# Another place for tile 5's transposed scores, and a written-out order of work, in a fused attention and softplus-FFN kernel

## The chip, the cores and the metric

One core of a Trainium2 chip runs the whole program. The metric is the device time of one launch in microseconds (us), as the median of several runs. The engines are named PE (TensorE), DVE (VectorE), ACT (ScalarE), POOL (GpSimd) and SP (SyncE, which here only issues DMAs).

## The reference, cut to what matters

```python
B, H, S, D = 8, 8, 576, 64          # chunks of 64 along S
scores = matmul(q_c, k_c.T) / sqrt(D)
attn = exp(scores - max(scores)); attn = attn / (sum(attn) + 1e-09)
x = matmul(attn, v_c)               # -> x (4608 x 512)
h = x @ w_in                        # w_in 512 x 2048
g = softplus(h)
out = g @ w_out                     # w_out 2048 x 512
```

All of it is float32; only chunks on the diagonal are computed.

## The kernel before, in words

**Matmuls in parts.** Each float32 factor of the FFN is split into a high and a low part, and three products (hi·hi, hi·lo, lo·hi) take the place of one. The weights arrive raw and are decoded once, in 32 units u: `w_load` (L309), `w_top` (L325), `w_low`, `w_add`, `w_hi` and `w_lo`. Raw weights pass through a ring of three buffers. The first units decode into `stage` (L257), four buffers called `wib`, each of which holds four units of 512 columns.

**Attention.** The 4608 tokens are 36 tiles i of 128. Tiles 0 to 3 are prepared on PE at the start. For the others, VectorE transposes q into a `qe` buffer and k into a `ka` buffer (`blk_t`, L539, tasks Tq and Tk; two `ka` buffers in all). PE computes the scores (`blk_s`, L556), VectorE takes the maximum and subtracts it (max, sub), ScalarE does the exponential, and VectorE or GpSimd the division. The probabilities must then be transposed: for most tiles VectorE does it wholly (`blk_e4`). Tile 5 is one of the few others: VectorE transposes 32x32 blocks with one instruction (`blk_e`, L575, task Te5), whose output lies in the tile's own key buffer `ka`, and eight DMAs of SP's queue move the blocks to their places in `eT` (`blk_swap`, L593, task swap5). PE then multiplies `eT` with v (L653), ScalarE writes the high part of x (xh) and VectorE the low part (xl).

**Bursts.** From tile 4 on PE does attention in bursts between FFN blocks: `burst` (L672) does the values of an earlier tile and the scores of a later one, once for each of a pair. Burst 8 has the values of tile 4 and the scores of tile 6 in its first half (B8_0), the values of tile 5 and the scores of tile 7 in its second (B8_1). Each half takes one of two `pa` banks of PSUM, which the first GEMM's outputs take in turn with it.

**FFN.** Nine blocks m of 512 tokens, sixteen slices fc of the hidden width. For the first three blocks each pair (m, fc), numbered g, is G1 (`gemm1`, L681), softplus on ScalarE (`sp_g`, L704, task sp), high part (hi), low part (lo) and G2 (`gemm2`, L911). The other six go in three supers of two blocks, whose G1 is done by seven products P0 to P6 for each pair of slices, in a Strassen-like scheme: VectorE and GpSimd combine results (`mix`), ScalarE copies some of them out of PSUM (`hold`, L868, tasks s1, e) and takes the softplus of others (`soft`, L895), and what cannot be used at once is spilled to memory (`spill_store`, L900). Final passes multiply the spilled part.

**The order.** Tasks are registered with `Plan.add`, each with its engine, cost, needs and urgency. `Plan.order` (L60) plays through these costs and chooses the order of each engine's instructions by urgency; `Plan.emit` (L146) then moves single tasks by two hand-written lists. An engine runs its instructions in that order. `keep_warm` (L421) puts matmuls of the identity matrix, whose result nobody reads, ahead of a task where the play-through leaves PE a gap early on:

```python
for _ in range(int(FILL * (plan.gap - 0.6) / 0.23)):
    nc.tensor.matmul(dst[:, :P], ident, ident, start=True, stop=True)
```

Tile 7's key transpose Tk7 writes into the buffer that tile 5's scores lie in until swap5 has moved them, so its needs hold swap5 (L1403):

```python
keep = [f"S{FIRST_BLK - 1}"] if ps == F else [f"Te{i - 2}" if n == "q" else swapped[i - 2]]
```

Of the kernel before, what the change touches and what calls it, by code (L numbers as in the profile page):

```python
# [33 lines left out]
class Plan:  # L34


    CROSS = 0.15
    OWN = 0.08
    TABLE = 1.28
    RATE = 265e3  # L40
    FLYING = 8
    AHEAD = 3.2
    WARM_UNTIL = 90.0
    HOLD = 0.55
    HOLD_FROM = 120.0

    def __init__(self, **pools):
        self.tasks, self.gap = {}, 0.0
        self.pools = {n: (c, []) for n, c in pools.items()}

    def add(
        self, name, eng, cost, fn, needs=(), urg=0.0, table=None, take=(), kb=0, slack=0.0, after=(), port=False, parts=1,
        late={}, room={}
    ):
        self.tasks[name] = dict(
            name=name, eng=eng, cost=cost, fn=fn, needs=list(needs) + list(after), after=set(after), urg=urg, table=table,
            take=take, kb=kb, slack=slack, seq=len(self.tasks), port=port or eng == "POOL", parts=parts, late=late, room=room,
        )

    def order(self):  # L60
        T = self.tasks
        kids, left, ready = {}, {}, {}
        for t in T.values():
            left[t["name"]] = len(t["needs"])
            for n in t["needs"]:
                kids.setdefault(n, []).append(t["name"])
        fin, issued, free, tab, dma_free, port = {}, {}, {}, None, 0.0, 0.0
        wait, landed = {}, {}
        times = [0.0]

        def known(t):
            r = t["slack"] if not t["needs"] else 0.0
            for n in t["needs"]:
                if n in t["after"]:
                    r = max(r, issued[n])
                    continue
                same = T[n]["eng"] == t["eng"] and not T[n]["kb"]
                lat = (0.0 if t["eng"] == "PE" else self.OWN) if same else self.CROSS + t["slack"]
                r = max(r, fin[n] + lat - t["late"].get(n, 0.0))
            ready[t["name"]] = r  # L80
            wait.setdefault(t["eng"], []).append(t)
            heapq.heappush(times, r)

        def has_room(t, now):
            for at, (pool, _) in enumerate(t["take"]):
# [11 lines left out]
        out = []  # L97
# [1678 lines left out]
```

## Time and profile before

| what | value |
|---|---|
| median of 3 runs | 822.53 us (821.55 to 823.56) |
| span of the profiled execution | 818.6 us |
| runs' median less that span | 3.9 us |
| PE busy | 809.0 us, 99% of the span |
| VectorE, ScalarE, GpSimd busy | 563.6, 391.4, 406.6 us |
| granted PE clock, mean | 0.998 |

The profiled execution is known by its span, from its first to its last instruction. A busy PE is not yet a PE at its peak: filler matmuls count as busy, and records of pipelined matmuls overlap, so that start times tell more than idle times. Line numbers are those of the kernel before.

### The profile page before, as it was taken

The numbers are of one execution on the slowest core, as the hardware profiler recorded it, in microseconds if no ns is written. First come the engines' busy times: TensorE is split into PE (matmuls) and PEld (weight loads), VectorE is DVE, ScalarE is ACT, GpSimd is POOL, SyncE is SP. The second block draws the span as 40 slices with busy tenths as digits, with TensorE's granted clock in tenths as the row PEclk, the third lists the DMA queues.
The fourth block names the chain that finished last, engine by engine and source line by source line (L and its number), as shares of the span: only waits on it lengthen the run. The fifth ranks groups of instructions, "written<-read, shape, count | busy, mean of one in ns | idle before, by whom it ended". The sixth has DMA issues, their size and how long they took to land.

```text
span 818.6 us, 16629 instructions
## 1 busy us (share of the span) xinstructions
PE 809.0 (99%) x6186; PEld 687.5 (84%) x6186; DVE 563.6 (69%) x914; ACT 391.4 (48%) x635; POOL 406.6 (50%) x512
## 2 busy tenths in 40 slices
PE   9999999999999999999999999999999999999997
PEld 7787888888888888888888888888888888999997
DVE  3998985357557687376769887376784646798773
ACT  4877765444443564354446545363542434443431
POOL 1555569776988643867857474336204550000000
PEclk9999999999999999999999999999999999999999
DMA  9987767764475455898897589886529998953421
GB/s 221 238 218 199 210 159 216 226 147 123 90 190 125 114 149 199 223 265 251 213 235 201 164 266 313 235 240 210 182 100 305 345 369 323 413 186 128 134 76 52
DMA packets 216482, 168.90 MB, mean 206 GB/s; under 512 B 153936, under 2 KB 186704, under 8 KB 215504
## 3 DMA queue, kind: packets, MB, share of 16 engines
q1 hardware_dynamic: 201648, 117.75, 50.0%
q0 software_dynamic: 14208, 49.56, 20.0%
q8 instruction: 49, 0.80, 0.4%
q10 hardware_dynamic: 544, 0.52, 0.2%
q14 instruction: 33, 0.27, 0.1%
HBM read 115.87 MB, written 50.86 MB: 204 GB/s over the span
## 4 chain that ended last, share of the span: by engine, by line
PE 88%; DMA 3%; DVE 3%; POOL 2%; ACT 2%; SPq 1%; issue 1%; DVEq 0%; POOLq 0%; ACTq 0%
PE po L922 28%; PE pa L863 21%; PE pa L690 14%; PE pa L1065 8%; PE po L1065 6%; PE po L863 5%; PE pa L653 2%; PE pa L565 1%; PE po L423 1%; DMA raw<-in_moe_w_in_dram 1%; DMA xa<-in_q_dram 1%; DMA tails<-xa 1%; DMA raw<-in_moe_w_out_dram 1%; SPq L534 0%; DVE wib L889 0%
## 5 line engine op out<-in xcount | busy, mean ns | idle before, releaser
L922 PE MATMUL po<-late,g_hi 128*128 128x512 f32 x360 | 110.3, 393 | 0.0
L863 PE MATMUL pa<-wib,xb 128*128 128x512 f32 x360 | 85.9, 392 | 0.0
L863 PEld LDWEIGHTS pa<-wib,xb 128*128 128x128 f32 x360 | 66.9, 188 | 15.8 <-ACT wib L869 1.8
L922 PEld LDWEIGHTS po<-late,g_hi 128*128 128x128 f32 x360 | 66.7, 188 | 14.6 <-DVE late L376 0.3
L863 PE MATMUL pa<-wi_hi,xb 128*128 128x512 f32 x240 | 73.9, 389 | 0.0
L922 PE MATMUL po<-wo_hi,g_hi 128*128 128x512 f32 x192 | 72.1, 394 | 0.0
L922 PE MATMUL po<-wo_hi,g_lo 128*128 128x512 f32 x192 | 71.4, 391 | 0.2 <-DVE g_lo L714 0.2
L922 PE MATMUL po<-wo_lo,g_hi 128*128 128x512 f32 x192 | 71.2, 390 | 0.0
L922 PE MATMUL po<-late,g_lo 128*128 128x512 f32 x192 | 70.9, 390 | 0.0
L706 ACT ACTIVATE u<-pa 128x512 f32<-128x512 f32 (+1 forms) x48 | 28.3, 589 | 83.0 <-PE pa L690 76.5
L818 POOL DMA_DIRECT2D xb<-scratch x58 | 35.9, 620 | 60.7 <-PE pa L863 57.8
L889 DVE TENSOR_TENSOR wib<-wib,pa 128x512 f32<-128x512 f32 x64 | 44.0, 687 | 28.9 <-PE pa L863 16.7
L897 ACT ACTIVATE ends<-pa 128x512 f32<-128x512 f32 x40 | 24.0, 599 | 78.6 <-PE pa L863 41.4
L863 PEld LDWEIGHTS pa<-wi_hi,xb 128*128 128x128 f32 x240 | 45.1, 188 | 9.7 <-issue 0.3
L589 DVE STREAM_TRANSPOSE eT<-qe 32x256 f32<-32x256 f32 x112 | 48.9, 436 | 2.6
L889 POOL TENSOR_TENSOR wib<-wib 128x512 f32<-128x512 f32 x32 | 42.0, 1311 | 17.1 <-ACT wib L869 16.4
L869 ACT COPY wib<-pa 128x512 f32<-128x512 f32 x52 | 29.7, 587 | 43.3 <-PE pa L863 43.3
L889 DVE TENSOR_TENSOR wib<-pa,wib 128x512 f32<-128x512 f32 x24 | 16.6, 690 | 45.8 <-ACT ends L897 23.8
L690 PE MATMUL pa<-xb,wib 128*128 128x512 f32 x192 | 46.5, 390 | 0.3 <-DVE wib L376 0.2
L863 PE MATMUL pa<-wi_lo,xb 128*128 128x512 f32 x120 | 46.7, 389 | 0.1
L714 POOL TENSOR_TENSOR g_lo<-u,g_hi 128x512 fp32r<-128x512 f32 x23 | 31.0, 1347 | 24.6 <-ACT g_hi L710 24.5
L922 PEld LDWEIGHTS po<-wo_hi,g_lo 128*128 128x128 f32 x192 | 36.0, 188 | 8.5 <-DVE g_lo L714 1.0
(370 smaller groups left out, 2075.7 us busy)
## 6 DMA issues: line engine op xcount, KB each, us to landing
xb<-scratch POOLq DMA_DIRECT2D x38, 512.0 KB, 5.6
spill<-ends SPq DMA_DIRECT2D x35, 512.0 KB, 5.5
xb<-scratch POOLq DMA_DIRECT2D x20, 768.0 KB, 7.0
ends<-spill SPq DMA_DIRECT2D x21, 512.0 KB, 3.3
out_dram<-raw SPq DMA_DIRECT2D x34, 256.0 KB, 3.4
raw<-in_moe_w_in_dram SPq DMA_DIRECT2D x16, 512.0 KB, 5.2
raw<-in_moe_w_out_dram SPq DMA_DIRECT2D x16, 512.0 KB, 4.6
scratch<-ends SPq DMA_DIRECT2D x16, 512.0 KB, 3.4
```

The lines of the kernel that those rows point to most:

```text
L589: nc.vector.transpose(live["eT", i][d : d + BL, tb], e[s : s + BL, 1 - tb])
L653: nc.tensor.matmul(pa[o, a, col : col + C], vt[r, 4 * j + 2 * h2 + c2, :], eT[r, :, 4 * c2 + 2 * j + h2, :], start=True, stop=True,)
L690: nc.tensor.matmul(ph, wt[:, c, :], x[:, ts_, c, :], start=(n == 0), stop=(n == 3 * KC - 1))
L706: nc.scalar.activation(w["u"], w["ph"], AF.Softplus)
L714: (nc.gpsimd if pool else nc.vector).tensor_tensor(w["lo"], w["u"], w["hi"].bitcast(F32), op=ALU.subtract)
L818: on("ring").dma_start(to[:, here], src[:, cut])
L863: nc.tensor.matmul(w["bank"][BANK[k]], wts[:, q, c, :], x[:, c, :], start=k < NX and c + n == 0, stop=c == 1 and n == 2, skip_group_check= ...
L869: nc.scalar.copy(tmp_of(n), w["bank"][n])
L889: (nc.gpsimd if what in MIX_POOL and w["s"] < LAST else nc.vector).tensor_tensor(out, a, b, op=op)
L897: nc.scalar.activation(u_tiles(j)[i], src, AF.Softplus)
L922: nc.tensor.matmul(pos[w["m"]][t], terms[n][0][:, j * P : (j + 1) * P], terms[n][1], start=(w["first"] and n == 0), stop=n == 2 and w["last"],
L1065: nc.tensor.matmul(f_bank(k)[:, t * HW : (t + 1) * HW], x[:, t * P : (t + 1) * P], wt, start=j == n == t == 0, stop=j == 7 and n == 2 and ...
```

## The change

Three things change. Tile 5's transposed scores (Te5) are written into the first 512 columns of the third staging buffer, and swap5 reads them there; Tk7 now needs the second half of burst 4 (the last reader of tile 5's key) in place of swap5. Te5 needs the decoded units of that buffer to be done, and one later weight step that writes there needs swap5. Second, the play-through and all urgencies are gone: a string `ISSUED` names all tasks in one order, which is each engine's order. Third, keep-warm matmuls are counted by a table instead of from the gaps of the play-through.

```diff
     def keep_warm(dst):
-        for _ in range(int(FILL * (plan.gap - 0.6) / 0.23)):
+        for _ in range(plan.warm):
             nc.tensor.matmul(dst[:, :P], ident, ident, start=True, stop=True)
-        plan.gap = 0.0
+        plan.warm = 0
...
     def blk_s(i, pa):
...
+        ea = stage[EA_STAGE[i]][:, :DM] if i in EA_STAGE else ea
         live["eA", i] = ea.rearrange("p (u h k) -> p u h k", u=2, h=H)
...
+    EA_STAGE = {5: 2}
...
                 keep = [f"S{FIRST_BLK - 1}"] if ps == F else [f"Te{i - 2}" if n == "q" else swapped[i - 2]]
+                if n == "k" and i - 2 in EA_STAGE:
+                    keep = [f"B{at_of[ps - 1]}_{i % 2}"]
...
+                staged = [f"w_{a_}{u_}" for a_ in ("hi", "lo") for u_ in range(4 * EA_STAGE[i], 4 * EA_STAGE[i] + 4)] if i in EA_STAGE else []
+                plan.add(f"Te{i}", "DVE", 0.65, partial(blk_e, i), [f"norm{i}"] + staged)
...
+    for i, n in EA_STAGE.items():
+        name = f"w_hi{of_in[HALF_FC + 4 * (n // 2)]}"
+        MOVED.append((name, {"needs": plan.tasks[name]["needs"] + [f"swap{i}"]}))
...
-    plan.emit(MOVED, BEHIND, AHEAD, in_turn)
+    WARM = {'T0': 15, 'S0': 3, 'E2': 3, 'V2': 2}
+    ISSUED = """
...
+    plan.emit(ISSUED.split(), MOVED, WARM, in_turn)
```

PE's order around burst 8, before (L690 is the first GEMM, L653 the values, L565 the scores, L423 the keep-warm matmuls, L922 the second GEMM):

```order
L690 MATMUL pa_963<-xb_370,wib_953 128x512 x4
L653 MATMUL pa_983<-eT_893,xa_105 64x64 x16
L565 MATMUL pa_983<-ka_957,qe_951 64x64 x16
L423 MATMUL pa_1044<-ident_86 128x128 x6
L653 MATMUL pa_1044<-eT_938,xa_105 64x64 x16
L565 MATMUL pa_1044<-ka_1039,qe_978 64x64 x16
L922 MATMUL po0_542<-wo_hi_101,g_hi_949 128x512
```

And with the change, where L568 is the first GEMM, L531 the values, L442 the scores and L800 the second GEMM:

```order
L568 MATMUL pa_966<-xb_370,wib_920 128x512 x4
L531 MATMUL pa_993<-eT_890,xa_105 64x64 x16
L442 MATMUL pa_993<-ka_981,qe_964 64x64 x16
L531 MATMUL pa_1042<-eT_928,xa_105 64x64 x16
L442 MATMUL pa_1042<-ka_988,qe_959 64x64 x16
L800 MATMUL po0_531<-wo_hi_101,g_hi_955 128x512
```

The six keep-warm matmuls between the halves of burst 8 are gone. Nothing else differs in PE's order from the first instruction to the last, and SP's order is the same except that swap5 reads `wib` instead of `ka`.

VectorE's order around tile 7's key, before (L541 is a key or query transpose, L345 a `w_add`, L610 a maximum, L615 its subtraction, L376 a `w_lo`, L670 an xl step; `ka_1039<-xa_105` is Tk7, `xa_1097<-pa_983` is xl4):

```order
L376 TENSOR_TENSOR wib_954<-ends_106,wib_953 128x512
L376 TENSOR_TENSOR wo_lo_102<-ends_106,wo_hi_101 128x512
L541 STREAM_TRANSPOSE qe_978<-xa_105 128x512
L345 ISA ends_106<-ends_106 128x1024 x2
L541 STREAM_TRANSPOSE ka_1039<-xa_105 128x512
L345 ISA ends_106<-ends_106 128x1024
L610 TENSOR_REDUCE mx_1102<-pa_983 128x8
L615 TENSOR_TENSOR qe_951<-pa_983,mx_1102 128x512
L376 TENSOR_TENSOR late_1023<-ends_106,late_1022 128x512
L670 TENSOR_TENSOR xa_1097<-pa_983,xa_1096 128x4x2x64
```

And with the change (L418, L222, L488, L493, L253 and L548 in the same roles; `ka_988<-xa_105` is Tk7, `xa_1090<-pa_993` is xl4):

```order
L222 ISA ends_106<-ends_106 128x1024
L418 STREAM_TRANSPOSE ka_981<-qk_116 128x512
L222 ISA ends_106<-ends_106 128x1024
L418 STREAM_TRANSPOSE ka_988<-xa_105 128x512
L253 TENSOR_TENSOR late_991<-ends_106,late_990 128x512
L488 TENSOR_REDUCE mx_1093<-pa_993 128x8
L548 TENSOR_TENSOR xa_1090<-pa_993,xa_1089 128x4x2x64
L493 TENSOR_TENSOR qe_964<-pa_993,mx_1093 128x512
```

Tk7 stands one step ahead of the `w_lo` into `late` in place of three, with tile 6's transposes just ahead of it, and xl4 stands ahead of the subtraction of tile 6 and of the first maximum of tile 7, where it stood behind the subtraction and a `w_lo`.

ScalarE's order in the third super at the end of its second pair, before (L869 is a hold, L897 a softplus, L1042 a cast; `wib_3547<-pa_6864` is the hold of the next pair, `po1_6808` and `po2_6818` are this pair's last products):

```order
L897 ACTIVATE ends_106<-wib_3547 128x512 x2
L869 COPY wib_3547<-po1_6808 128x512
L869 COPY wib_3547<-pa_6864 128x512
L897 ACTIVATE ends_106<-po1_6808 128x512
L897 ACTIVATE ends_106<-po2_6818 128x512
L897 ACTIVATE ends_106<-wib_3547 128x512 x2
L1042 CAST eT_6906<-raw2_6772 128x256
L1042 CAST eT_6907<-raw2_6772 128x256
```

And with the change (L747 is a hold, L775 a softplus; `wib_3541<-pa_6861` is that hold):

```order
L775 ACTIVATE ends_106<-wib_3541 128x512 x2
L747 COPY wib_3541<-po1_6802 128x512
L775 ACTIVATE ends_106<-po2_6813 128x512
L775 ACTIVATE ends_106<-wib_3541 128x512
L775 ACTIVATE ends_106<-po1_6802 128x512
L747 COPY wib_3541<-pa_6861 128x512
L775 ACTIVATE ends_106<-wib_3541 128x512
L920 CAST eT_6903<-raw2_6758 128x256
```

The hold stands behind three softplus steps of the pair before it, where it stood ahead of all four.

## Rows read from the trace of the kernel before

**Rows 1.** The profile page: its first line, and busy us of the engines.

```profile
span 818.6 us, 16629 instructions
...
PE 809.0 (99%) x6186; PEld 687.5 (84%) x6186; DVE 563.6 (69%) x914; ACT 391.4 (48%) x635; POOL 406.6 (50%) x512
```

**Rows 2.** Table of stretches: start:end, length, busy us (instructions) by engine, PE clock, DMA share, GB/s.

```profile
0.00:40.00 40.00, 36.98 (x434) 31.56 (x435) 25.02 (x46) 25.04 (x46) 14.35 (x21) 1.00 1.01 227
...
615.00:693.00 78.00, 78.00 (x347) 64.38 (x346) 38.77 (x64) 26.36 (x49) 31.75 (x50) 1.00 0.95 337
```

**Rows 3.** Timeline of PE around burst 8: start, us, engine, line, op, [idle before <-releaser].

```profile
71.99 2.11 PE L690 MATMUL pa<-xb,wib 128*128 128x512 f32 x8 [0.17 <-DVE wib L376]
74.03 0.69 PE L653 MATMUL pa<-eT,xa 64*64 64x64 f32 x32
74.55 0.65 PE L565 MATMUL pa<-ka,qe 64*64 64x64 f32 x32
75.12 1.60 PE L423 MATMUL pa<-ident 128*128 128x128 f32 x12
76.66 0.69 PE L653 MATMUL pa<-eT,xa 64*64 64x64 f32 x32
77.58 0.69 PE L565 MATMUL pa<-ka,qe 64*64 64x64 f32 x32 [0.22 <-DVE ka L541]
78.20 1.19 PE L922 MATMUL po<-wo_hi,g_hi 128*128 128x512 f32 x4
...
80.15 1.07 PE L922 MATMUL po<-wo_hi,g_lo 128*128 128x512 f32 x4
81.34 2.98 PE L690 MATMUL pa<-xb,wib 128*128 128x512 f32 x12
```

**Rows 4.** Timeline of PE: the next burst (117.12 to 119.14), and G2 at 95.04.

```profile
95.04 2.19 PE L922 MATMUL po<-late,g_hi 128*128 128x512 f32 x8
...
117.12 0.69 PE L653 MATMUL pa<-eT,qk 64*64 64x64 f32 x32
...
119.14 2.11 PE L922 MATMUL po<-late,g_hi 128*128 128x512 f32 x8
```

**Rows 5.** Tile eT, 60 to 82 us: swap5's issues on SP's queue, and issue to landing.

```profile
L600 SPq DMA_DIRECT2D eT<-ka x8: 507/588/602, 69.9 to 74.7; - x8
...
DMA to landing us min/median/max: 1.8/3.7/5.0
```

**Rows 6.** Timeline of VectorE around burst 8 (same columns).

```profile
76.81 0.71 DVE L541 STREAM_TRANSPOSE ka<-xa 128x512 f32<-128x512 f32 x1 [2.10 <-DMA eT<-ka]
...
80.51 0.68 DVE L670 TENSOR_TENSOR xa<-pa,xa 128x512 fp32r<-128x512 f32 x1
```

**Rows 7.** Timeline of SP's queue ahead of swap5 (same columns).

```profile
69.39 0.39 SPq L317 DMA_DIRECT2D raw<-in_moe_w_in_dram  x1
```

**Rows 8.** Timeline of PE at 416 and at 454 us (same columns).

```profile
416.36 0.69 PE L565 MATMUL pa<-ka,qe 64*64 64x64 f32 x32 [0.38 <-DVE ka L541]
...
454.66 0.50 PE L922 MATMUL po<-wo_hi,g_lo 128*128 128x512 f32 x1 [0.22 <-DVE g_lo L714]
```

**Rows 9.** Timeline of VectorE at 452 us (same columns).

```profile
452.79 1.22 DVE L836 TENSOR_TENSOR wib<-xa 128x1024 f32<-128x1024 f32 x1
```

**Rows 10.** Timeline of ScalarE in the third super (same columns).

```profile
637.21 1.09 ACT L897 ACTIVATE ends<-po 128x512 f32<-128x512 f32 x2 [0.25 <-DMA spill<-ends]
...
655.51 0.59 ACT L869 COPY wib<-pa 128x512 f32<-128x512 f32 x1 [2.05 <-PE pa L863]
```

**Rows 11.** Timeline of PE in the third super (same columns).

```profile
637.52 0.63 PE L863 MATMUL pa<-wi_hi,raw 128*128 128x512 f32 x2
```

**Rows 12.** Timeline of ScalarE around burst 8 (same columns).

```profile
74.20 0.60 ACT L706 ACTIVATE u<-pa 128x512 f32<-128x512 f32 x1 [0.21 <-PE pa L690]
...
75.72 0.78 ACT L330 CAST ends<-raw 128x512 f16<-128x512 bf16 x1
```

**Rows 13.** Timeline of PE at 24 us (same columns).

```profile
24.25 0.66 PE L475 MATMUL po<-ident,late 128*128 128x128 f32 x4 [1.23 <-DVE late L640]
```

More of the change, by code (lines that the diff above doesn't have):

```diff
@@ L1 @@
-import heapq
 import math
@@ L34 @@
 class Plan:
[L37 to L45, printed above, removed]
     def __init__(self, **pools):
-        self.tasks, self.gap = {}, 0.0
+        self.tasks, self.warm = {}, 0
         self.pools = {n: (c, []) for n, c in pools.items()}
     def add(
-        self, name, eng, cost, fn, needs=(), urg=0.0, table=None, take=(), kb=0, slack=0.0, after=(), port=False, parts=1,
-        late={}, room={}
+        self, name, eng, cost, fn, needs=(), table=None, take=(), kb=0, after=(), parts=1, late={}, room={}
@@ L54, in add, with emit @@
     ):
         self.tasks[name] = dict(
-            name=name, eng=eng, cost=cost, fn=fn, needs=list(needs) + list(after), after=set(after), urg=urg, table=table,
-            take=take, kb=kb, slack=slack, seq=len(self.tasks), port=port or eng == "POOL", parts=parts, late=late, room=room,
+            name=name, eng=eng, fn=fn, needs=list(needs) + list(after), after=set(after), take=take,
+            kb=kb, parts=parts, table=table, cost=cost, late=late, room=room,
         )
-    def order(self):
+    def emit(self, order, moved=(), warm={}, around=lambda t: t["fn"]()):
@@ L61, in order @@
         T = self.tasks
[L62 to L82, printed above, removed]
@@ L142, in order @@
-        if len(out) != len(T):
-            raise ValueError(f"never ready: {[n for n in T if n not in fin][:12]}")
-        return out, fin
-    def emit(self, moved=(), behind=(), ahead=(), around=lambda t: t["fn"]()):
-        T, out = self.tasks, self.order()[0]
-        start, lanes, gaps, last = {}, {}, {}, 0.0
-        for now, t in out:
-            start[t["name"]] = now
-            lanes.setdefault(t["eng"], []).append(t["name"])
-            if t["eng"] == "PE":
-                gaps[t["name"]] = now - last if now < self.WARM_UNTIL else 0.0
-                last = now + t["cost"]
@@ L180, in can @@
             return True
[L182 to L189 removed]
+        for name in order:
+            t = T[name]
+            if name in done or not can(t):
+                raise ValueError(f"out of order: {name}")
+            done.add(name)
             for pool, rel in t["take"]:
                 used[pool].append(rel)
[L192 removed]
+            self.warm = warm.get(name, 0)
             around(t)
+        if len(done) != len(T):
+            raise ValueError(f"left out: {[n for n in T if n not in done][:12]}")
 @with_exitstack
@@ L1365, in chunked_attention_softplus_ffn @@
     for key, (pv, ps) in bursts.items():
-        d, at = due(key), tag(key)
+        at = tag(key)
         for n in range(2):
```

426 lines of the change are left out of this document (214 added, 212 removed), and 8 rows, old and new, of the table BEHIND.

## The prediction, made before the changed kernel was run

> **What bounds the kernel now.** I read the page first, then a table of stretches, then the timelines of the stretches that the change touches. The page says that TensorE (PE) is busy for 809.0 of the 818.6 us of the profiled span [rows 1]. The table of stretches says that most of the rest lies in the first 40 us, which the change leaves nearly alone, and that in the stretch of the third super PE is busy for all of 78.00 us while the DMA engines are at a share of 0.95 [rows 2]. So the kernel can gain only what PE now spends on filler or on waits, and the reader should look for those by start times, not by the idle column: a 128x512 matmul is recorded as 0.39 us long, but a run of four adds 0.23 us each (2.98 us for twelve), so that up to 0.16 us of a stall hides behind an overlapping record.
>
> The largest such place is burst 8 [rows 3]. PE does the values of tile 4 and the scores of tile 6 at 74.03, then 1.60 us of keep-warm matmuls at 75.12, then the values of tile 5 at 76.66, the scores of tile 7 at 77.58, and leaves for G2 at 78.20. That is 4.17 us. The next burst has the same four parts without filler and takes 119.14 - 117.12 = 2.02 us [rows 4]. So 2.15 us is the most that burst 8 can give back.
>
> **The change part by part.** The measurement of this kernel tells about 0.2% (1.65 us) from no change. The profiled span is 818.6 us and the median of the runs is 822.53 us, so 3.9 us lie around it; I take these as unchanged and work in differences.
>
> *The six keep-warm matmuls* leave PE's list. They cost 1.54 us from 75.12 to 76.66, but this is not yet a gain: what stands behind them needs eT of tile 5, which swap5's eight DMAs fill. Their last issue is at 74.7 and one of them takes 1.8 us to land at the least [rows 5], so the last cannot be there before 76.5; VectorE's transpose of tile 7's key, which waited for exactly this, began at 76.81 [rows 6]. Between 76.5 (lower bound of the landing) and 76.7 I take 76.5, since PE's own start at 76.66 already had the data. The filler therefore stood in a wait that stays, and its removal by itself gives 76.66 - 76.5, some 0.15 us. Below nothing the term can only go by the clock, which is a rival.
>
> *The wait of Tk7 for swap5* goes, since the scores that swap5 reads now lie in a staging half. In the old order Tk7 ran at 76.81 after 2.10 us of idling [rows 6], so the scores of tile 7 came at 77.58 instead of at 76.66 + 0.52 (the first half of the burst has its scores 0.52 after its values). In the new order Tk7 needs only the second half of burst 4, long done, and its place on VectorE comes earlier, so its key is there before 76.5. Values and scores together then take 75.12 - 74.03 = 1.09 us [rows 3], G2 starts at 76.5 + 1.09 = 77.6 instead of 78.20: **0.6 us** with the 0.15 above included. The wait that ends last is then swap5's landing, not Tk7. SP's list is the same in both kernels, swap5 stands behind a load at 69.39 [rows 7], and nothing that it is moved past is new.
>
> *The first stall of the stretch*, 0.17 us before 71.99 and some 0.3 more hidden in the start times, goes with VectorE's new order (its w_lo comes earlier), but I cost that at nothing: PE would only reach the wait for swap5 earlier. If swap5 landed sooner, it would be worth up to 0.4 us.
>
> *G1 of block 9 at 81.34.* G2's four matmuls from 80.15 end their turn at 80.15 + 4 x 0.23 = 81.06; PE waits 0.28 us more, for the bank that the subtraction xl4 frees (80.51 to 81.19 [rows 6]; PE's rows are in [rows 3]). In the new order xl4 stands ahead of the score subtraction (0.6 us earlier), so the wait goes: **0.3 us**.
>
> *Other stalls in the reordered stretches.* G2 at 95.04 takes 2.19 us for eight matmuls [rows 4], where 0.39 + 7 x 0.23 = 2.0 is due; what it waits for is late on VectorE, whose decode steps are in another order now, and I give the new order that 0.2 us (bounds 0 and 0.2). At 454.66 a G2 matmul starts 0.61 after its neighbour instead of 0.23, because g_lo stood behind steps of 1.22 us [rows 8, 9]. The new order puts g_lo between single steps: **0.4 us** (bounds 0 and 0.6). The stall at 416.36 [rows 8] waits for a key transpose that waits for a load; the order of the loads is the same, so nothing.
>
> *The third super.* ScalarE now runs the hold of pair 2 behind two or three softplus steps instead of ahead of them. In the old order the softplus at 637.21 began only when a spill store had landed [rows 10], and PE took up the product that needs the held bank at about 637.7 (the second of the two matmuls from 637.52 [rows 11]). A softplus there starts 0.5 after the one before (1.09 us for two), the hold takes 0.6. If in the new order only the last softplus needs the landing, the hold is done at 637.2 + 0.5 + 0.6 = 638.3, 0.6 us after PE wants it; if the last two do, at 638.8, 1.1 us after. Bounds: 0, if the store lands 0.6 us earlier, and 1.1. I take **0.7 us lost** here, near the first, since one landing is what the old row shows, and nothing for the next two pairs: at 655.51 ScalarE had idled 2.05 us before the hold, for PE [rows 10], so there is room for a softplus ahead of it.
>
> **Sum:** -0.6 - 0.3 - 0.2 - 0.4 + 0.7 = -0.8 us. Span 817.8, time 822.5 - 0.8 = **821.7 us**, 0.1% faster: less than a measurement can tell.
>
> **The rivals.**
>
> *The whole burst comes back.* If ScalarE's new order frees a raw buffer earlier, the loads ahead of swap5 on SP's queue go out earlier and swap5 with them. For it: SP is held by landings, not by its own work, and the queue is the whole of the bound. Against it: the loads just ahead of it wait for buffers whose readers wait for landings in turn. If all eight were there by 75.1, burst 8 would give its 2.15 us; with the 0.3, 0.2 and 0.4 and no loss at the hold this is -3.05: 819.5 us. It decides at an issue of the last swap DMA before 73.3.
>
> *Holds behind spill stores: slower.* Holds stand behind softplus steps in three pairs of the third super, and the DMA share there is 0.95 [rows 2]. If each softplus waits for a store, each pair loses the 1.1 us worked out above. 3 x 1.1 = 3.3, against gains of 1.5: +1.8, 824.3 us. It decides where the landing comes later than 1.6 us (two softplus steps and the hold) before PE wants the bank, in all three. For it: the landing at 637.21 was already that late. Against it: PE works ahead in the other pairs. The same sort of wait stands at burst 8: the softplus sp8, at 74.20 before, now stands behind a w_top which ran at 75.72 [rows 12]; PE needs sp8's bank for the second half of the burst, and 75.72 plus 0.8 and 0.6 would be 77.1, 0.6 later than swap5. That alone would take the first term away: +2.4 instead of +1.8, the end of this rival.
>
> *The clock falls without the filler.* PE would wait for swap5 from about 75.1 to 76.5, 1.4 us. The rows show an idle time of 1.23 us before 24.25 [rows 13], in a stretch whose granted clock is 1.00 (2.4 GHz) all through [rows 2], so I count on no fall. If it fell to 1.2 GHz until G2 of block 8 is through, the 4.4 us from 76.66 to 81.06 would take twice as long: 4.4 - 0.8 = +3.6, 826.1 us. "TensorE: Matmul & The Clock Gate", section "What's actually happening", in the Trainium skill, has the throttled clock as the default which activity releases, so that by it idle PE time can cost the clock; by it alone the filler was worth keeping, and the trace has no fall after an idle time as long as this one.
>
> *The change doesn't do what it says.* If Tk7's place on VectorE or the load of tile 7's key holds the scores as long as swap5 did, G2 still starts at 78.2, and the rest is +-0.5: 822.5 us.
>
> **How the numbers follow.** The forecast (a small net gain) has 0.52, the whole burst 0.22, the slower one by holds 0.12, the clock 0.03, no effect 0.11. Of the forecast's 0.52 I count 0.08 as passing 1.65 us (bounds at their best: -0.6 -0.3 -0.2 -0.6 = -1.7), the rest as within. So faster 0.22 + 0.08 = 0.30, same 0.44 + 0.11 = 0.55, slower 0.12 + 0.03 = 0.15. The range leaves out about one in ten on each side: down to the whole burst's 819.5, up to 823.8, most of the way to the slower rival.
>
> **What would show it.** Right: no L423 row in burst 8, PE idle before the values of tile 5 with swap5's landing (not VectorE's key transpose) as what ended it, G2 near 77.6, G1 of block 9 without a wait, and a wait of PE near 637 for ScalarE's hold. Wrong: PE's second half of burst 8 begins before 76 (the whole burst) or after 77 (sp8), a granted clock under 1.00 after burst 8, or waits for the hold in more than one pair. The forecast as a whole is wrong if the runs lie under 820.9 or over 824.2.

## The result, and the profile after

The changed kernel is slower: 830.66 us in the median of 6 runs (826.71 to 835.82), against 821.70 us for the kernel before in the same comparison (6 runs, 821.02 to 823.56). The ratio is 1.0103, 95% interval 1.0082 to 1.0125. The prediction had 821.7 us and a range up to 823.8. The page of the profiled execution, to set beside [rows 1]: its span is 829.6 us, 11.0 more than before. The six runs differ in their mean granted clock: the one at 1.000 took 826.71 us, still 5.0 us over before, and the one at 0.991 took 835.82, so the clock can be no more than a part of the loss.

```profile
span 829.6 us, 16519 instructions
...
PE 812.2 (98%) x6174; PEld 688.2 (83%) x6174; DVE 561.0 (68%) x914; ACT 390.3 (47%) x635; POOL 404.5 (49%) x512
...
PE 78%; DMA 8%; DVE 5%; ACT 3%; issue 3%; POOL 2%; SPq 0%; DVEq 0%; POOLq 0%; ACTq 0%
```

The chain line is the short form of what happened: PE makes up 78% of the chain and transfers 8%, where the page before had PE at 88% and transfers at 3%. Two rows of the table of stretches (columns as in [rows 2]) show the places, and the clock of one of them:

```profile
40.00:90.00 50.00, 46.13 (x364) 37.22 (x363) 41.27 (x66) 32.44 (x53) 25.85 (x25) 0.93 0.78 200
...
460.00:615.00 155.00, 150.39 (x1068) 121.79 (x1067) 108.04 (x168) 70.14 (x111) 66.49 (x86) 1.00 0.75 220
```

From 40 to 90 us PE is busy for 46.13 us, and its mean granted clock is 0.93; from 460 to 615 us it is busy for 150.39 of 155 us, where the kernel before had 154.92. The start times of the same PE work in both traces give the account; where a time is called late, it is against the same matmul in the trace of before, of one execution each. PE's timeline around burst 8, to set beside [rows 3] (L531 values, L442 scores, L800 second GEMM, L568 first GEMM):

```profile
74.02 0.69 PE L531 MATMUL pa<-eT,xa 64*64 64x64 f32 x32
75.39 0.69 PE L442 MATMUL pa<-ka,qe 64*64 64x64 f32 x32 [0.68 <-DVE ka L418]
79.08 1.63 PE L531 MATMUL pa<-eT,xa 64*64 64x64 f32 x29 [2.99 <-ACT u L584]
...
81.59 2.07 PE L800 MATMUL po<-wo_hi,g_hi 128*128 128x512 f32 x4
...
86.31 2.89 PE L568 MATMUL pa<-xb,wib 128*128 128x512 f32 x12
```

Burst 8 begins at the same time as before (74.02 against 74.03). The keep-warm matmuls are gone, as the order said. But tile 6's scores wait 0.68 us for a key transpose, and tile 5's values start at 79.08, not at 76.5: PE idles 2.99 us for ScalarE's softplus `u` (sp8). Then G2's twelve matmuls take 86.31 - 81.59 = 4.72 us, where before [rows 3] the same twelve took 81.34 - 78.20 = 3.14. The first GEMM of block 9 starts at 86.31 instead of 81.34: 4.97 us late. Of these, 2.42 lie ahead of tile 5's values (79.08 against 76.66), and 2.55 in the work from there on. The table of short stretches shows why the matmuls are slow:

```profile
76.00:78.00 2.00, 0.09 (x8) 0.00 (x0) 0.84 (x2) 1.83 (x4) 0.09 (x1) 1.00 0.69 198
78.00:79.00 1.00, 0.00 (x0) 0.00 (x0) 0.91 (x2) 1.00 (x2) 1.00 (x2) 0.90 0.14 37
79.00:80.00 1.00, 0.79 (x14) 0.63 (x18) 1.00 (x1) 0.97 (x3) 0.99 (x2) 0.50 0.64 98
...
85.00:86.00 1.00, 1.00 (x4) 0.76 (x4) 0.96 (x3) 0.39 (x1) 1.00 (x2) 0.69 0.29 42
86.00:88.00 2.00, 2.00 (x11) 1.63 (x10) 1.63 (x3) 0.30 (x1) 1.05 (x2) 1.00 0.94 273
```

PE does next to nothing from 76 to 79 us, and from 79 us on the granted clock is 0.50 (1.2 GHz), until it comes back between 85 and 86. What PE waited for can be read on three other engines. SP's queue first, to set beside [rows 7], with swap5's issues and landings, to set beside [rows 5]:

```profile
72.45 0.39 SPq L194 DMA_DIRECT2D raw<-in_moe_w_in_dram  x1
72.94 5.37 SPq L478 DMA_DIRECT2D eT<-wib  x8
...
L478 SPq DMA_DIRECT2D eT<-wib x8: 507/588/597, 72.9 to 77.8; - x8
...
DMA to landing us min/median/max: 1.8/3.5/5.0
```

The load ahead of swap5 goes out at 72.45 instead of 69.39, and swap5 begins at 72.94; its last issue is at 77.8 and no landing took under 1.8 us, so that its last landing cannot be before about 79.6. ScalarE's timeline, to set beside [rows 12]:

```profile
75.84 0.76 ACT L207 CAST ends<-raw 128x512 f16<-128x512 bf16 x1 [2.48 <-DMA raw<-in_moe_w_out_dram]
...
77.80 0.78 ACT L207 CAST ends<-raw 128x512 f16<-128x512 bf16 x1 [0.17 <-DMA raw<-in_moe_w_in_dram]
78.45 0.57 ACT L584 ACTIVATE u<-pa 128x512 f32<-128x512 f32 x1
```

The softplus (L584) starts at 78.45, right behind a weight step (77.80) that had to wait for that late load. VectorE's timeline, to set beside [rows 6] (L222 is a w_add, L418 here Tk7):

```profile
77.16 0.69 DVE L222 CUSTOM_DVE_ANT_0 ends<-ends 128x1024 uint16<-128x1024 uint16 x1 [1.82 <-ACT ends L217]
77.76 0.71 DVE L418 STREAM_TRANSPOSE ka<-xa 128x512 f32<-128x512 f32 x1
```

Tk7, no longer held by swap5, runs at 77.76, later than before (76.81): it stands behind a w_add that waits 1.82 us for ScalarE. So three things came late for the second half of burst 8: Tk7 (done at 78.5), the softplus that frees its bank (79.0), and swap5 (79.6 and later).

The rest of PE's timeline, at the places of [rows 8, 11] and two more:

```profile
421.02 0.65 PE L442 MATMUL pa<-ka,qe 64*64 64x64 f32 x32
...
458.52 0.39 PE L800 MATMUL po<-wo_hi,g_lo 128*128 128x512 f32 x1
...
530.96 0.73 PE L741 MATMUL pa<-wi_hi,xb 128*128 128x512 f32 x2 [2.10 <-DVE wib L767]
...
647.34 0.73 PE L741 MATMUL pa<-wi_hi,raw 128*128 128x512 f32 x2
...
687.25 0.73 PE L741 MATMUL pa<-wi_hi,raw 128*128 128x512 f32 x2 [0.35 <-ACT wib L747]
```

Against the same work before, 421.02 is 4.66 us late (416.36 [rows 8]) and 458.52 is 3.86 late (454.66 [rows 8]): from 81 to 454 us PE gains back 1.1 us. Then it goes the other way. The product at 530.96 is 7.04 us late (523.92 before), the one at 647.34 is 9.8 late (637.52 [rows 11]), the one at 687.25 is 11.4 late (675.82 before). The greatest single step behind burst 8 is the one ahead of 530.96, where PE idles 2.10 us for VectorE's combining step. VectorE there, after and then before (L418 and L541 transpose, L767 and L889 combine):

```profile
529.62 0.71 DVE L418 STREAM_TRANSPOSE qe<-raw 128x512 f32<-128x512 f32 x1 [6.29 <-DMA raw<-in_k_dram]
530.26 0.65 DVE L767 TENSOR_TENSOR wib<-wib,pa 128x512 f32<-128x512 f32 x1
```

```profile
518.01 1.48 DVE L889 TENSOR_TENSOR wib<-wib,pa 128x512 f32<-128x512 f32 x2 [0.66 <-ACT ends L897]
519.41 0.70 DVE L541 STREAM_TRANSPOSE qe<-raw 128x512 f32<-128x512 f32 x1
```

In the changed order a query transpose stands ahead of the combining step c11, and it waits 6.29 us for a load; c11 needs nothing from it, but VectorE does its work in order, so c11 waits as well, and PE behind it. Before, c11 (the second of the two steps from 518.01) came first, and the transpose behind it (519.41) did not wait for its load.

The load itself is late, and more than PE is. SP's queue, after and then before (`xa<-spill` is the task ul0_5, `qk<-in_k` a key load that goes out ahead of tile 33's):

```profile
488.76 0.32 SPq L783 DMA_DIRECT2D xa<-spill  x1
...
509.57 8.28 SPq L411 DMA_DIRECT2D qk<-in_k_dram  x8
```

```profile
480.48 0.32 SPq L905 DMA_DIRECT2D xa<-spill  x1
...
501.78 5.78 SPq L534 DMA_DIRECT2D qk<-in_k_dram  x8
```

The spill load goes out 8.28 us later than before, where PE is 3.8 us late, and what stands behind it on the queue is late with it. It goes out when the low-part steps lo70 and lo71 are done with the buffer that it fills. VectorE there, after (lo70 is the step at 486.42) and then before (both steps in one row):

```profile
484.79 0.69 DVE L767 TENSOR_TENSOR wib<-wib,pa 128x512 f32<-128x512 f32 x1 [1.72 <-ACT wib L747]
...
486.42 2.31 DVE L592 TENSOR_TENSOR g_lo<-xa,g_hi 128x512 fp32r<-128x512 f32 x1
```

```profile
478.88 1.57 DVE L714 TENSOR_TENSOR g_lo<-xa,g_hi 128x512 fp32r<-128x512 f32 x2
```

In the changed order lo70 stands behind the combining step e_1_1, which waits 1.72 us for a hold of ScalarE, and behind block transposes; it ends at 488.73, and the load goes out at 488.76.

### The profile page after: what moved, and what is told of

Its sections match the earlier page's. It is cut to its first block, busy times and chain, and to the rows that moved or that the text cites. A ratio compares the mean times of both kernels' runs of the same rounds, so it can differ in the third digit from the quotient of the medians.

```text
span 829.6 us, 16519 instructions
## 1 busy us (share of the span) xinstructions
PE 812.2 (98%) x6174; PEld 688.2 (83%) x6174; DVE 561.0 (68%) x914; ACT 390.3 (47%) x635; POOL 404.5 (49%) x512
## 4 chain that ended last, share of the span: by engine, by line
PE 78%; DMA 8%; DVE 5%; ACT 3%; issue 3%; POOL 2%; SPq 0%; DVEq 0%; POOLq 0%; ACTq 0%
PE po L800 26%; PE pa L741 16%; PE pa L568 14%; PE pa L943 8%; PE po L943 6%; DMA spill<-ends 2%; PE po L741 2%; PE pa L531 2%; DVE wib L767 2%; PE pa L442 2%; DMA raw<-in_moe_w_in_dram 1%; DMA tails<-raw 1%; DMA xa<-spill 1%; ACT ends L775 1%; DMA out_dram<-raw 1%
## 5 line engine op out<-in xcount | busy, mean ns | idle before, releaser
L800 PE MATMUL po<-late,g_hi 128*128 128x512 f32 x360 | 110.1, 392 | 0.0
L800 PEld LDWEIGHTS po<-late,g_hi 128*128 128x128 f32 x360 | 66.9, 188 | 14.1
L800 PE MATMUL po<-wo_hi,g_hi 128*128 128x512 f32 x192 | 73.0, 400 | 0.0
L800 PE MATMUL po<-wo_hi,g_lo 128*128 128x512 f32 x192 | 71.9, 393 | 0.3 <-DVE g_lo L592 0.3
L800 PE MATMUL po<-wo_lo,g_hi 128*128 128x512 f32 x192 | 72.1, 395 | 0.0
L800 PE MATMUL po<-late,g_lo 128*128 128x512 f32 x192 | 71.0, 390 | 0.2 <-POOL g_lo L592 0.2
L584 ACT ACTIVATE u<-pa 128x512 f32<-128x512 f32 (+1 forms) x48 | 28.3, 589 | 88.6 <-PE pa L568 84.3
L767 DVE TENSOR_TENSOR wib<-wib,pa 128x512 f32<-128x512 f32 x64 | 43.9, 687 | 37.5 <-PE pa L741 23.2
L775 ACT ACTIVATE ends<-pa 128x512 f32<-128x512 f32 x40 | 23.3, 598 | 81.9 <-PE pa L741 45.9
L767 POOL TENSOR_TENSOR wib<-wib 128x512 f32<-128x512 f32 x32 | 42.6, 1330 | 29.3 <-ACT wib L747 28.4
L747 ACT COPY wib<-pa 128x512 f32<-128x512 f32 x52 | 29.5, 587 | 39.6 <-PE pa L741 34.2
L568 PE MATMUL pa<-xb,wib 128*128 128x512 f32 x192 | 46.2, 389 | 0.0
L767 DVE TENSOR_TENSOR wib<-pa,wib 128x512 f32<-128x512 f32 x24 | 16.5, 686 | 41.2 <-ACT ends L775 17.9
L800 PEld LDWEIGHTS po<-wo_hi,g_lo 128*128 128x128 f32 x192 | 36.3, 189 | 9.3 <-DVE g_lo L592 1.7
```

Of the source, the lines that this page charges most:

```text
L568: nc.tensor.matmul(ph, wt[:, c, :], x[:, ts_, c, :], start=(n == 0), stop=(n == 3 * KC - 1))
L584: nc.scalar.activation(w["u"], w["ph"], AF.Softplus)
L747: nc.scalar.copy(tmp_of(n), w["bank"][n])
L767: (nc.gpsimd if what in MIX_POOL and w["s"] < LAST else nc.vector).tensor_tensor(out, a, b, op=op)
L775: nc.scalar.activation(u_tiles(j)[i], src, AF.Softplus)
L800: nc.tensor.matmul(pos[w["m"]][t], terms[n][0][:, j * P : (j + 1) * P], terms[n][1], start=(w["first"] and n == 0), stop=n == 2 and w["last"],
```

## The experiments

Task names are those of the two orders: w_top, w_low, w_add, w_hi, w_lo decode a weight unit, sp and hi are softplus and high part of a block, c11, e, f combine products (e too, which the description of the kernel before lists with the holds), lo is a low part, ul loads a spilled operand on SP's queue, s1 is a hold, soft a softplus of a super, Tq and Tk are transposes, ring loads operands for PE on GpSimd's queue. PE's and SP's orders are the same in all kernels, except for the six keep-warm matmuls; only the orders of VectorE, ScalarE and GpSimd are exchanged, piece by piece, as lists of the same tasks. Ratios are against the kernel before in the same comparison.

**The parts of the change: place, filler, early order, late order.**

```diff
 e1_place_only: the changed kernel's file with
-ISSUED = the changed order; WARM without B8_1
+ISSUED = the order of before, task by task; WARM = {..., 'B8_1': 6}
 e2_place_no_filler: as e1, with
-WARM = {..., 'B8_1': 6}
+WARM without B8_1
```

> The order of before, written out, with its six keep-warm matmuls; only the place of tile 5's transposed scores and the needs of Tk7 are changed. If the loss of 9 us comes from the order (my theory: steps of ScalarE and VectorE that PE needs now stand behind steps that wait for a landing), this is within 0.5 us of before, 821.5 to 822, with Tk7 at about 74.7 and the scores of tile 7 0.4 us earlier. If it comes from the new place (Te5 or swap5 late), burst 8 ends over 1 us later than 78.2 and the time is 823 or more.

> As the run with the place alone, but without the six keep-warm matmuls of burst 8. My theory (an idle time under 1.5 us does not cost the clock here, what cost it in the changed kernel was the wait of 3 us) gives a granted clock of 1.00 after burst 8 and 0 to 0.6 us less than with them: 821 to 822. If the filler is what keeps the clock, it falls to 1.2 GHz (0.50) in the first microseconds after burst 8 as in the changed kernel and the time is 2 to 4 us more: 824 to 826.

Measured: e1 821.22 us, ratio 0.9998 (0.9981 to 1.0014); e2 821.66 us, 1.0002 (0.9989 to 1.0016). Neither can be told from before, so the new place and the lost filler cost nothing by themselves. In e1 Tk7 ran at 74.64 and the scores of tile 7 followed the values by 0.52 us. PE's timeline of e2 in burst 8:

```profile
74.46 0.65 PE L442 MATMUL pa<-ka,qe 64*64 64x64 f32 x32
75.26 0.30 PE L531 MATMUL pa<-eT,xa 64*64 64x64 f32 x2
76.44 0.63 PE L531 MATMUL pa<-eT,xa 64*64 64x64 f32 x27 [0.88 <-DMA eT<-wib]
...
77.52 1.20 PE L800 MATMUL po<-wo_hi,g_hi 128*128 128x512 f32 x4
...
81.22 2.97 PE L568 MATMUL pa<-xb,wib 128*128 128x512 f32 x12 [0.66 <-ACT ends L217]
```

PE waits for swap5 in two pieces (75.26 shows two matmuls of the first, then 0.88 us of idling), G2 leaves at 77.52, and the granted clock stays at 1.00 in every stretch from 70 to 84 us. The prediction's own scene, with 77.6, came true in this kernel, not in the changed one. The gain did not last: G1 of block 9 starts at 81.22 (81.34 before [rows 3]), since PE now waits 0.66 us there. The row names a step of ScalarE; by the times it is VectorE's xl4, which stands where it stood before and runs from 80.39 to 81.07.

```diff
 e3_early_of_before: the changed kernel, up to about 130 us
-VectorE, ScalarE, GpSimd: the changed order
+VectorE, ScalarE, GpSimd: the order of before
 e4_late_of_before: the changed kernel, from about 455 us on
-VectorE, ScalarE, GpSimd: the changed order
+VectorE, ScalarE, GpSimd: the order of before
```

> The changed kernel with the order of before in the decode and attention stretch up to about 130 us (VectorE, ScalarE, GpSimd), and its own order from there on. If the two losses are separate, the 4.8 us around burst 8 are gone, the gains at 416 and 450 us (1.2 us) and the losses after 487 us (7 us) stay: 825 to 828. If the late losses only follow from PE being late by 5 us, they go too: 820 to 822.

> The changed kernel with the order of before from the end of the first super on (about 455 us), and its own order ahead of that. If the two losses are separate, the loss around burst 8 stays (4.8 us, with the clock at 0.50 for some 6 us) and the 7 us after 487 are gone: 824 to 826, PE with no wait over 0.5 us after 460 us. If the late losses follow from the early one, they stay here too: 829 to 832.

Measured: e3 828.40 us, ratio 1.0088 (1.0053 to 1.0123); e4 834.68 us, 1.0150 (1.0125 to 1.0176). In e3 the late losses are there without the early one, so they do not follow from it. Its largest wait of PE is the one for c11 again:

```profile
529.70 0.72 PE L741 MATMUL pa<-wi_hi,xb 128*128 128x512 f32 x2 [3.15 <-DVE wib L767]
```

e3 lies just above its first branch. e4 missed its expectation. Where its two orders are joined, from 472 to 497 us, PE loses some 12 us that neither kernel has, and e4 does not compute the same values as the others, so its time as a whole says nothing. What can be read is the part behind the join: from 511 us to the end PE stays at the same distance from the trace of before (16.4 us at 494 and at the end), with no late loss.

**The early order and the clock.**

```diff
 e5_early_alone: as e2, up to about 130 us
-VectorE, ScalarE, GpSimd: the order of before
+VectorE, ScalarE, GpSimd: the changed order
 e6_early_sp8_first: as e5, on ScalarE
-w_hi17 w_top19 sp8 hi8 xh4
+w_hi17 sp8 hi8 w_top19 xh4
 e9_sp8_first_filler: as e6, and e10_early_filler: as e5, each with
-WARM without B8_1
+WARM = {..., 'B8_1': 6}
```

> The place without filler and the order of before, with the changed kernel's own order only in the decode and attention stretch up to about 130 us. If that order alone makes the early loss (my theory), burst 8 waits 2 us or more, the granted clock falls to 0.50 for some microseconds, and the time is 3.5 to 5.5 us over before: 825 to 827. If the early loss needs anything later or was an accident of one profile, it is within 1.5 us of before.

> As e5_early_alone, with one step of ScalarE moved: the softplus of block 8 and its high part stand ahead of the weight step that waits for a load. The trace of the changed kernel has the last of swap5's landings no earlier than 79.5, 0.4 us behind the point at which the softplus let PE go (79.08), so if the loads on SP's queue, 3 us late, are what holds burst 8, this gains under 0.7 us on e5. If the softplus behind the load is the cause (the end of my slower rival), it gains 2 us or more and the clock stays at 1.00.

Measured: e5 822.66 us, ratio 1.0004 (0.9983 to 1.0025); e6 822.83 us, 1.0015 (0.9994 to 1.0036). e5 lost far less than the 3.5 us expected, and moving the softplus gained nothing that can be measured. But the clock did fall, in the profiled runs of both. The short stretches of e5:

```profile
76.00:78.00 2.00, 1.10 (x31) 0.99 (x34) 1.91 (x3) 1.97 (x5) 2.00 (x3) 0.80 0.41 100
78.00:80.00 2.00, 2.00 (x47) 1.78 (x41) 2.00 (x5) 0.38 (x2) 1.35 (x2) 0.50 0.97 346
...
82.00:84.00 2.00, 2.00 (x10) 1.68 (x9) 1.97 (x4) 1.27 (x2) 1.88 (x2) 1.00 0.17 23
```

and PE's waits in e6, where the softplus is early:

```profile
75.49 0.30 PE L531 MATMUL pa<-eT,xa 64*64 64x64 f32 x2 [1.05 <-ACT g_hi L588]
76.38 0.63 PE L531 MATMUL pa<-eT,xa 64*64 64x64 f32 x27 [0.59 <-DMA eT<-wib]
```

With the softplus early, PE still waits for swap5 (the second of these rows), and the clock falls to 0.50 there too. The single runs tell more than the medians. In e5, the two runs with a mean granted clock of 0.999 took 818.79 and 819.41 us; the other eight, at 0.995 to 0.997, took 820.97 to 825.22. In e6 three runs at 0.999 took 819.96 to 821.87, seven at 0.994 to 0.997 took 820.48 to 826.73. So the early order without filler often loses the clock, and the runs that keep it are no slower than before.

> As e6_early_sp8_first, with the six keep-warm matmuls of burst 8 back. In the single runs of e5 and e6 the time goes with the mean granted clock: 818.8 to 820.3 us at 0.999, 823 to 827 at 0.994 to 0.996. If the clock lost after burst 8 is what costs there (new theory: the early order itself is the better one, the missing filler makes it lose the clock in most executions), the filler, whose bank the softplus frees early here, holds every run at 0.998 or more and the median is 819 to 820.5, ratio 0.996 to 0.999. If late loads are what costs and the clock only falls with them, the median stays at 822 to 824.

> As e5_early_alone (the softplus of block 8 stays behind the weight step that waits for a load), with the six keep-warm matmuls back. They write into the bank that this softplus frees, so PE idles ahead of them as long as in e5 (1.3 us there) and does them only then. If the idle time ahead of the softplus is what loses the clock, some runs still fall to 0.995 and the median is 821.5 to 823.5. If any matmul before the values is enough, all runs stay at 0.998 or more and the median is 820 to 821.

Measured: e9 821.41 us, ratio 0.9999 (0.9988 to 1.0010), ten of twelve runs at a clock of 0.998 or more; e10 823.17 us, 1.0013 (0.9998 to 1.0027), eight of twelve at 0.996 or 0.997. With the filler the clock holds in most runs if the softplus frees the filler's bank first, and in a third of them if the softplus stands behind the weight step. PE in e10:

```profile
77.37 2.48 PE L300 MATMUL pa<-ident 128*128 128x128 f32 x12 [1.79 <-ACT u L584]
```

The idle time comes ahead of the filler, and the filler itself then takes 2.48 us instead of 1.60 [rows 3]. In e9 the clock came nearly as expected, the time did not: the median is that of before, not 819 to 820.5. The new theory, that the early order is the better one once the clock holds, is not borne out by it.

**The late order.**

```diff
 e7_mix_before_transpose: the changed kernel, on VectorE
-f2_1_3 Tq33 c11_1_3 lo76
+f2_1_3 c11_1_3 Tq33 lo76
 e8_middle_alone: as e2, from about 310 to 470 us
-VectorE, ScalarE, GpSimd: the order of before
+VectorE, ScalarE, GpSimd: the changed order
```

> The changed kernel with two neighbouring steps of VectorE exchanged: the combining step c11 of the fourth pair of the second super ahead of the query transpose of tile 33, as in the order of before. If that step, stuck behind a transpose whose load lands at 529.6, is what PE waits for at 530.96, its 2.1 us and the wait for the hold at 533 (0.5 us) go: 2 to 3 us under the changed kernel, 827 to 829. If PE was late there for another reason (its operands' loads), the wait is put down to something else and under 0.5 us is gained.

> The place without filler and the order of before, with the changed kernel's own order only from about 310 to 470 us, where the two traces show the changed kernel ahead (0.4 us at 416, 0.4 at 449, 0.4 at 455). If the gains there stand by themselves, 0.8 to 1.2 us under before: 820.3 to 821. If they only came because PE was late by 5 us when it got there, within 0.4 us of before.

Measured: e7 828.15 us, ratio 1.0066 (1.0040 to 1.0092), 2.5 us under the changed kernel's median, by one exchange of two neighbours. The two intervals overlap a little (1.0082 to 1.0125 for the changed kernel), so the size is rough, but the trace shows the mechanism. VectorE in e7:

```profile
519.29 1.48 DVE L767 TENSOR_TENSOR wib<-wib,pa 128x512 f32<-128x512 f32 x2
526.40 0.71 DVE L418 STREAM_TRANSPOSE qe<-raw 128x512 f32<-128x512 f32 x1 [5.63 <-DMA raw<-in_k_dram]
```

The transpose still idles 5.63 us for its load, and nobody waits for it now: c11 is done at 520.8, the second of the two steps from 519.29. Not all of it lasts: in the stretch that lies at 511 to 530 us before, PE loses 3.25 us in the changed kernel and none in e7, but from 511 to the end 6.8 and 5.7. e8 missed: 824.74 us, 1.0039 (1.0025 to 1.0052), slower where a gain was expected. Its gains at 416 and 455 us are there (0.56 and 0.38 us against before), but PE waits at places that the changed kernel's trace did not show. Two of them, and VectorE ahead of the second:

```profile
411.04 4.36 PE L741 MATMUL pa<-wib,xb 128*128 128x512 f32 x18 [1.13 <-DMA xb<-scratch]
...
521.85 1.65 PE L741 MATMUL pa<-wib,xb 128*128 128x512 f32 x6 [1.66 <-DVE wib L767]
```

```profile
520.51 0.71 DVE L418 STREAM_TRANSPOSE ka<-qk 128x512 f32<-128x512 f32 x1 [6.16 <-DMA qk<-in_k_dram]
```

At 411 PE waits for operands which GpSimd's queue loads (ring), and again at 517. The wait at 521.85 is of the same sort as that for c11: a combining step behind a transpose whose load is late. Here the steps of VectorE stand as before, where the same transpose (511.55) and the combining step behind it (513.31) cost PE nothing. What is new is the load, and the late load comes with the middle order. In the six profiles with the changed order of VectorE up to there (the changed kernel, e3, e7, e8, e13, e15), ul0_5 goes out 3.2 to 4.5 us later than PE's own lateness explains, and PE loses 1.2 to 7.3 us in the stretch that lies at 505 to 535 us before; in the ten others (e1, e2, e5, e6, e9 to e12, e14, e16) it goes out within 0.2 us of it, and PE loses nothing there. No run moves lo70 alone, so the step is read from the traces; that the middle order makes these loads late is what the sixteen show.

```diff
 e11_late_alone: as e1, from about 485 us on
-VectorE, ScalarE, GpSimd: the order of before
+VectorE, ScalarE, GpSimd: the changed order
 e12_holds_alone: as e1, on ScalarE in the third super (five pairs, such as)
-s1_2_2 soft10_2_1 soft01_2_1 soft11_2_1
+soft01_2_1 soft11_2_1 soft10_2_1 s1_2_2
```

> The place, the filler and the order of before, with the changed kernel's own order only from about 485 us on (second half of the second super, third super, final passes). Of the 9 us that the changed kernel loses, 0.8 came with the early order and 2.9 with the middle one, so if losses add up this loses 4 to 6 us: 825.5 to 828, with waits of PE for VectorE's combining steps near 525 us and for ScalarE's holds after 635 us. If the late losses need the middle's order ahead of them, under 2 us.

> The place, the filler and the order of before, with only ScalarE's order of holds and softplus steps in the third super taken from the changed kernel (in five pairs the hold s1 goes behind one to three softplus steps). The prediction priced one such pair at 0.7 us (bounds 0 and 1.1) and the others at nothing: 822 to 823. The slower rival has 1.1 us in each of three pairs: 824.5 to 825.5. The traces of the changed kernel and of e7 show steps of 0.5 to 2.1 us near 637, 652 and 676 us.

Measured: e11 825.62 us, ratio 1.0043 (1.0028 to 1.0059), in the range expected, but not by the wait expected: in its profiled run the transpose ahead of c11 waits 1.92 us instead of 6.29, and PE loses nothing there. e12 821.94 us, 1.0002 (0.9988 to 1.0015), not to be told from before. The holds do cost a wait in single pairs, but not in the pair that the prediction priced. PE in e12:

```profile
678.98 0.73 PE L741 MATMUL pa<-wi_hi,raw 128*128 128x512 f32 x2 [1.23 <-ACT wib L747]
```

This is the pair near 679 us; the one near 637 us shows no wait. Early, middle and late order alone lose 0.04, 0.39 and 0.43%, together 0.86%; the whole change loses 1.03% (0.82 to 1.25), so within the intervals the three add up. They do not act singly: the wait for c11 is in the kernels that have the middle and the late order (the changed kernel and e3), and not in e11.

**Which steps.**

```diff
 e13_middle_pool_before: as e8, with
-GpSimd: the changed order
+GpSimd: the order of before
 e14_late_without_two: as e11, with c11_1_3 ahead of Tq33 and s1 ahead of soft as before
 e15_four_put_back: the changed kernel, with sp8 hi8 ahead of w_top19, 'B8_1': 6,
   GpSimd's order of before, c11_1_3 ahead of Tq33, s1 ahead of soft
 e16_gains_only: as e1, with the changed order only for
+VectorE: w_lo18 max6 xl4 sub6 ... xl5, and Tq28 to xL1_6; ScalarE: exp26 to s0_1_1
```

> As e8_middle_alone (which lost 2.9 us), but with GpSimd's order of before: only VectorE's and ScalarE's middle order is the changed kernel's. In e8 PE waited 1.1 us at 411 and 0.7 us at 517 for operands (xb) that GpSimd loads and that it issues later in the changed order. If GpSimd's order is the cause, 1.5 us or more of the 2.9 go: 821 to 823. If VectorE's order is, the time stays at 824 to 825.5.

> As e11_late_alone (which lost 4.2 us), but with two pieces put back to the order of before: the combining step c11 ahead of the transpose of tile 33 on VectorE, and the holds of the third super ahead of the softplus steps on ScalarE. If these two make the late loss, 2.5 us or more of the 4.2 go: 821.5 to 823. If the loss is spread over the other steps, under 1.5 us go: 824 to 826.

> The changed kernel with five things put back: the softplus of block 8 ahead of the weight step, the six keep-warm matmuls, GpSimd's whole order, c11 ahead of the transpose of tile 33, and the holds ahead of the softplus steps. If the steps named by the traces are the causes, 6 us or more of its 9 us are gone: 821.5 to 824.5. If the loss is spread over all the rest of VectorE's and ScalarE's order, 826 to 829.

> The place, the filler and the order of before, with only those pieces of the changed order in which the traces showed it ahead: xl ahead of the score subtraction after burst 8 (0.3 us at 81), and VectorE's and ScalarE's order from about 410 to 460 us (0.4 us each at 416, 449 and 455). If they stand alone, 0.7 to 1.5 us under before: 820 to 820.8, ratio 0.998 to 0.999. If the gains are taken back by waits further on, within 0.4 us of before.

Measured: e13 827.87 us, ratio 1.0099 (1.0072 to 1.0126); e14 824.23 us, 1.0030 (1.0019 to 1.0041); e15 826.64 us, 1.0062 (1.0049 to 1.0075); e16 822.06 us, 1.0015 (1.0001 to 1.0030). All four missed the hopeful end; e14 and e15 came out by their other branch, e13 and e16 by neither. Taking GpSimd back to the order of before did not help the middle, if anything it is worse (only four runs, 824.48 to 833.23): GpSimd's changed order alone was not the cause, and in e13's profile ul0_5 is 3.2 us late against PE as in the others. Two thirds of the late loss stay when the two named pieces are put back (the intervals overlap, and one of the two, c11, had cost e11 nothing), and 0.62 of 1.03% of the whole when five are. The gains alone are no gain: in the profiled run of e16, the slowest of its twelve, PE waits 3.55 us for a key transpose at the very place where the changed kernel was ahead.

```profile
422.05 1.13 PE L442 MATMUL pa<-ka,qe 64*64 64x64 f32 x32 [3.55 <-DVE ka L418]
```

No kernel tried here beats the kernel before beyond the measurement.

## Why the prediction was wrong

**The step on swap5 failed.** The prediction took its landing at 76.5, the wait that should end last, from the old trace, since "SP's list is the same in both kernels", and had tile 7's key there before that. The list is the same, the times are not: in the changed kernel's profile the load ahead of swap5 went out 3.06 us later, Tk7 ran at 77.76, and the softplus at 79.02 and swap5 at 79.6 or later ended last. The prediction looked at moving loads once, for a gain (swap5 earlier, 0.22 of the chance), and gave lateness no term. How late swap5 is differs between executions, and 3 us is the far end: measured from the start of burst 8, swap5 begins 1.1 to 3.6 us ahead of it in the eight kernels with the changed early order (1.1 in the changed kernel), and 3.8 to 4.5 us ahead in the ten with that of before. So the order of the other engines moves the queue against PE; which of their steps does it is not shown. From the start of burst 8 to G1 of block 9 the eight take 1.8 us more than before in the median (0.96 to 4.99), the others 0.1 (-0.64 to 0.94). In the medians of the runs of e5 and e6 this is too small to tell.

**The terms of burst 8 were right where nothing else moved.** e2 gave G2 at 77.52 against the 77.6 of the prediction, and e1 showed Tk7 free at 74.64. That xl4's place would be worth 0.3 us at block 9 was right too: in e16, with xl4 ahead, G1 starts 0.92 us after G2's last four matmuls begin, where before it took 81.34 - 80.15 = 1.19 [rows 3], and without it e2 gave its gain back there.

**The rivals.** The softplus behind the weight step, which the prediction put at the far end of its slower rival, happened as described (79.0 instead of 77.1), but putting it first alone gained nothing that can be measured (e6), since swap5 was next. The clock rival (0.03) did happen, by the mechanism stated. Its price was 4.4 us for the work from tile 5's values to block 9; in the changed kernel this work took 86.31 - 79.08 = 7.23 us instead of 81.34 - 76.66 = 4.68 [rows 3], 2.55 more, and in e5 the eight runs that lost the clock are some 4 us slower than the two that held it. The argument against it, that 1.23 us of idling at 24 us had not cost the clock [rows 13], does not hold: e6 idled 1.05 and 0.59 us and lost it, e2 and e8 idled about as long and kept it. The rule in the Trainium skill ("TensorE: Matmul & The Clock Gate", section "What's actually happening"), that activity releases the clock and idling lets it go, agrees with the 0.50 that the stretch from 79 us shows, and with e9 and e10.

**The reordered rest was not priced.** This is the larger failure: 0.39% from the middle and 0.43% from the late order, 6.7 us together. The prediction went through the old trace for waits that the new order might remove, and found some: 0.4 us at 455, where the traces show 0.38, and 0.2 at 95 us, where they show some 0.3. (At 416, where it had expected 0, the changed kernel gains 0.56, but so, within 0.1, do e6, e10 and e11 with the order of before there, so the new order does not make it.) It looked for new waits only among the holds. There it took the wrong pair: 0.7 us at 637, where the trace after shows 0.1; the wait of a hold that shows in e12 is 1.23 us, at 679. It did not go through the new order for steps that PE needs and that now stand behind a step that waits for a transfer, nor for steps that SP's loads wait for. The exchange of c11 and Tq33 was there to be read in VectorE's order, and in the old trace the transpose of the same tile's key waited 1.32 us for its load at 523.30. The greatest loss that the traces name, 3.25 us of PE's time between 511 and 530 us, takes both: the pair, and a load that the move of lo70 had held up. The premise that failed is that of swap5 once more: "the order of the loads is the same, so nothing", as the prediction put it for the stall at 416.

**What stays open.** The rest of the loss is not traced to single steps. e14 and e15 show that the steps put back in them make less than half of it, and e8, e13 and e16 that waits appear at other places with each mixture. lo70, which the traces name for the late loads of the second super, was not put back in any of them. That the old order is a matched set, in which each engine's list fits the landings and the other lists, is what these runs suggest; that is argued, not shown. Whether filler with another place would let the early order keep its 819 us was not tried.

## What to carry to other kernels

When a change reorders in-order engines, read the new order for every step that the bounding engine needs and ask what now stands ahead of it; a step that waits for a transfer stops everything behind it, needed or not, and one such pair cost PE 3.25 us at its place here, though only because the load was late as well. Do not carry a transfer's landing time over from the old trace because its queue's order is the same: ask who frees the buffers that the queue waits for. And price a removed filler not by the wait it covers in the old trace but by the longest wait that could stand in its place.

## What the runs showed of the hardware

The granted clock stayed at 1.00 through a PE wait of 0.88 us between short bursts (e2) and through 1.40 and 0.71 us close together (e8). It fell to 0.50 after 2.99 us (the changed kernel), after 1.34 and 0.29 us in e5, and after 1.05 and 0.59 us in e6, so that waits of nearly the same length gave both. In these three PE had work again while it was at the lower level, and the clock was back at 1.00 by 86 us in the changed kernel and by 82 us in e5. Single runs of one kernel differ with it: in e5 from 818.8 us at a mean clock of 0.999 to 825.2 at 0.995.
